# Scores of an attention kernel: one full matmul of mixed products and one of 64 rows, with two heads' tiles in turns

## The chip, the cores and the metric

The kernel runs on one core of a Trainium2 chip. A core has five engines that run side by side and wait for each other through semaphores: TensorE (matmuls, PE in the profile, with its weight loads as PEld), VectorE (DVE), ScalarE (ACT), GpSimd (POOL) and SyncE (SP), which here issues the DMAs. The metric is the device time of one execution in microseconds (us); lower is better.

## The reference

Attention with normalised queries and keys, and an MLP with an ELU on its result:

```python
B, H, S, D = 8, 12, 448, 64            # batches, heads, sequence, head size
q_n, k_n = rmsnorm(q, g_q), rmsnorm(k, g_k)
scores = (q_n @ k_n.T) / 8             # per batch and head, 448 x 448
attn = softmax(scores)                 # with the row maximum taken off
x = (attn @ v)                         # heads side by side: 3584 x 768
h = x @ w_in                           # 768 x 2048
g = where(h > 0, h, exp(min(h, 0)) - 1)
out = g @ w_out                        # 2048 x 768
```

All inputs are float32.

## The kernel before

Matmuls run in float16. To keep the precision of float32, each operand is split in a high part (its float16 value) and a low part (what is left), and several products of parts are added up in PSUM.

The work goes by pairs of heads p, 48 in all (6 for each batch). For a pair, `load_qk` fetches queries and keys, the `qk_...` steps normalise them, and `k_high`, `q_high`, `k_low`, `q_low` write high and low parts side by side into the tile `t16`, whose slots (query or key, 7 blocks of 128 rows, high or low, 64 values) become partitions when `qk_transpose` (line 439) transposes them by DMA into `qkt`. There, entry 0 has the queries and entry 1 the keys, head after head, with the high part in partitions 0 to 63 and the low part in 64 to 127. `q_swap` (line 446) moves the two halves of the queries into entry 2 with their places exchanged, by two more DMAs.

Scores are made by `s_mm(T)` in tiles T of 128 query rows, 7 for a pair (896 rows). Six tiles have rows of one head; one straddles both and is made of 64 rows of each (`cuts`). The list `ORDER` says which chunk of rows a tile takes: here 0, 1, 2, 4, 3, 5, 6, so the straddling chunk 3 is the fifth. A tile takes two matmuls over all 128 partitions (line 554): queries in entry 0 against keys give high by high plus low by low, and the exchanged ones in entry 2 give the mixed products. For the straddling tile each of them is two matmuls with 64 output partitions. The result is in one of the PSUM banks `s0` to `s4`, chosen by `t_s(T)`: five in turns at first, four once the MLP needs `s4`.

A tile is then worked on in steps: `s_max` (VectorE, line 561), `s_exp` (ScalarE, 575), `s_z` (GpSimd, 579), `s_rec` (VectorE, 587), `s_hi` (ScalarE, 618) and `s_lo` (VectorE, 628), which write high and low probabilities and free the bank, and `s_tr` (638), a DMA that transposes them. In pairs 1, 3 and 5 TensorE does this turning instead (`s_pe`, 599; there the low part is line 625). `attend(p)` (658) multiplies by the values, in matmuls of 64 output partitions for each head, in turns.

The MLP (`mlp`, lines 743 and 757, 128 x 448 outputs, two high by part and one low by high product) is a stream of matmuls that is laid between the attention's. The order of all is written out by hand: a loop over half steps h runs, at each h, the steps that the table `SCHED` puts there, and then part of the MLP's stream, by the targets of `due(h)`. With two things on TensorE in a half step, the stream's share is divided around them: from `START` on, `s_mm(T + 1)` comes at the odd half steps, and `attend(p - 1)` right behind the straddling tile of pair p:

```python
        if ok(T + 1) and odd == (h >= START):
            mm.append(lambda: s_mm(T + 1))
        if r == 7 and 0 <= p - 1 < NP:
            mm = [lambda mm=mm: (*(fn() for fn in mm), attend(p - 1))]
```

The order in which each engine meets its instructions is the order of this loop. The steps of tile T stand at 2T and following half steps; `s_lo` has 2T + 4.5. `PB` is 42, the tiles of a batch, and `NJ` is 7. In the first batch's attention the weights are converted and split as well (`conv_in`, `conv_out`), and no MLP is there yet.

Of the kernel before, what the change touches and what calls it, by code (L numbers as in the profile page):

```python
# [13 lines left out]
AF = mybir.ActivationFunctionType  # L14
ALU = mybir.AluOpType
# [4 lines left out]
B, H, S, D = 8, 12, 448, 64  # L20
# [3 lines left out]
NJ = 2 * S // 128  # L24
NCHUNK = B * NPAIR * NJ
PB = NPAIR * NJ
# [6 lines left out]
def tile_attention_then_elu_mlp(ctx: ExitStack, tc: tile.TileContext, qk, v, v_scan, gg, w_in, w_out, out):  # L33
# [13 lines left out]
    nc = tc.nc  # L47
# [8 lines left out]
    def bank(name):  # L56
        return psum.tile([128, 512], F32, name=name)

    sb = [bank(f"s{i}") for i in range(5)]
# [2 lines left out]
    taken = 0  # L62

    def t_s(T):
        return sb[T % (5 if T < PB + (5 if PE_PAIRS else 0) else 4)]

    def t_mo():
        nonlocal taken
# [9 lines left out]
        out=neg, in0=ident, scalar1=-1.0, scalar2=None, op0=ALU.mult  # L78
# [3 lines left out]
        out=ident, in0=ident, scalar1=2.0**UP, scalar2=None, op0=ALU.mult  # L82
# [260 lines left out]
    nat, vt, qkt, pts, pss, p16s, stats = ({} for _ in range(7))  # L343
    st1, sqs, t16s = {}, {}, {}
# [72 lines left out]
        )  # L417

    def q_high(p):
        nc.scalar.activation(t16s[p][:, 0, :, 0], nat[p][:, 0], AF.Copy)  # L420

    def k_low(p):
        t = t16s[p][:, 1]
# [4 lines left out]
    def q_low(p):  # L428
        t = t16s[p][:, 0]
        eng = nc.gpsimd if p else nc.vector  # L430
        eng.tensor_tensor(
            out=t[:, :, 1], in0=nat[p][:, 0], in1=t[:, :, 0], op=ALU.subtract
        )

    def qk_transpose(p, i):
# [4 lines left out]
            out=qkt[p][:, i], in_=t16[:, i].rearrange("p j s d -> p (j s d)")  # L440
        )

    def q_swap(p):
        q = qkt[p]
        for a, z in ((64, 0), (0, 64)):
            nc.sync.dma_start(out=q[z : z + 64, 2], in_=q[a : a + 64, 0])

    def v_mult(p):
        n = vn[p]
# [85 lines left out]
    def cuts(j):  # L535

        a, z = j * 128, j * 128 + 128
        if z <= S:
            return [(0, 0, a, 128)]
        if a >= S:  # L540
            return [(1, 0, a - S, 128)]
        return [(0, 0, a, S - a), (1, S - a, 0, z - S)]


    ORDER = (0, 1, 2, 4, 3, 5, 6)

    def s_mm(T):
        p, j = divmod(T, NJ)
        ps = pss[T] = t_s(T)
        qq = qkt[p].rearrange("p t j n -> p t (j n)")  # L550
        for t in (0, 2):
            for h, r0, q0, n in cuts(ORDER[j]):
                lhs = qq[:, t, h * S + q0 : h * S + q0 + n]
                nc.tensor.matmul(  # L554
                    ps[r0 : r0 + n, :S], lhs, qq[:, 1, h * S : h * S + S],
                    start=(t == 0), stop=(t == 2),
                )

    def s_max(T):
        st = stats[T] = small("st", 3, bufs=6)  # L560
# [4 lines left out]
    def by_pe(T):  # L565


        return T // NJ in PE_PAIRS
# [35 lines left out]
    def turned(T):  # L604
        q0 = ORDER[T % NJ] * 128
        ps = pss[T][:CK].rearrange("p (c q) -> p c q", c=4)
        return ps, pt_pe[:, 0, :, q0 : q0 + 128], pt_pe[:, 1, :, q0 : q0 + 128]
# [24 lines left out]
    def s_tr(T):  # L632
        p, j = divmod(T, NJ)
        p16 = p16s.pop(T)
        for h, r0, q0, n in cuts(ORDER[j]):
            if 2 * p + h not in pts:
# [150 lines left out]
    for T in reversed(range(NCHUNK)):  # L787
        k = 2 if by_pe(T) else 0 if T < PB else 1
        hs = [2 * T + h for h in SCHED["tile"][k]]
        j = T % NJ  # L790
# [7 lines left out]
    for p in range(NP):  # L798
        k = p if p < 12 else 11
        put([h + HP * (p - k) for h in SCHED["qk"][k]], [  # L800
            (load_qk, p), (qk_square, p), (qk_sum, p), (qk_root, p), (qk_newton, p), (qk_norm, p),
            (k_high, p), (q_gain, p), (q_high, p), (k_low, p), (q_low, p), (qk_transpose, p, 0),
            (qk_transpose, p, 1), (q_swap, p),
        ])
        put([h + HP * (p - k) for h in SCHED["v"][k]], [
            (load_v, p), (v_mult, p), (v_high, p), (v_low, p), (v_shift, p), (x_high, p),
            (x_low, p),
        ])
    for b in range(B):
        k = min(b, 2)  # L810
# [8 lines left out]
    for b in range(B):  # L819
        k = min(b, 1)  # L820
# [23 lines left out]
    for h in range(H0, LAST):  # L844
        T, odd = divmod(h, 2)

        run_tasks(h - 0.5, 1)
        run_tasks(h - 0.5, 2)
        run_tasks(h, 0)
        ok = lambda t: 0 <= t < NCHUNK  # L850
        run_tasks(h, 1)
        want = due(h + 1)
        n = max(0, want - done)
        mm = []
        p, r = divmod(h, HP)
# [5 lines that stand above are left out]
        parts = len(mm) + 1  # L861
        for k in range(parts):
            for _ in range(n * (k + 1) // parts - n * k // parts):
                r = next(moe, None)
                done += 1
                if r:
                    steps_at(h + 1, enumerate(r))
            if k < len(mm):
                mm[k]()
        run_tasks(h, 2)  # L870
    h = LAST - 1
# [106 lines left out]
PE_PAIRS = (1, 3, 5)  # L978
# [42 lines left out]
```

## Time and profile before

| | |
|---|---|
| time, median of 3 runs | 1267.01 us (1266.6 to 1267.09) |
| profiled execution, first to last instruction (its own time; nothing else of it is told) | 1265.7 us |
| TensorE busy, and its weight loads | 94%, 58% |
| VectorE, ScalarE, GpSimd busy | 68%, 70%, 43% |
| share of the DMA engines | 73% |
| score matmuls of 64 output columns of weights, of 128 | 192, 576 |

In the views below, a row of a timeline has the start in us from the span's start, the length, the engine, the line of the kernel, the operation, what it writes and reads, the shape, and how many are merged (x4); brackets show idle time of the engine just before, and what ended it. For a matmul, 128\*64 means 128 rows (contracted) by 64 columns of weights. A matmul's length is from its start until its last result; the next may start long before that end. A row of windows has the stretch, its length, and busy times. In a row of waits, the three numbers are the total in us, the count, and the longest.

### The profile page before, as it was taken

The numbers are of one execution on the slowest core, as the hardware profiler recorded it, in microseconds if no ns is written. First come the engines' busy times: TensorE is split into PE (matmuls) and PEld (weight loads), VectorE is DVE, ScalarE is ACT, GpSimd is POOL, SyncE is SP. The second block draws the span as 40 slices with busy tenths as digits, with TensorE's granted clock in tenths as the row PEclk, the third lists the DMA queues.
The fourth block names the chain that finished last, engine by engine and source line by source line (L and its number), as shares of the span: only waits on it lengthen the run. The fifth ranks groups of instructions, "written<-read, shape, count | busy, mean of one in ns | idle before, by whom it ended". The sixth has DMA issues, their size and how long they took to land.

```text
span 1265.7 us, 21796 instructions
## 1 busy us (share of the span) xinstructions
PE 1194.4 (94%) x7150; PEld 732.5 (58%) x7150; DVE 855.3 (68%) x1913; ACT 879.8 (70%) x1889; POOL 538.9 (43%) x858
## 2 busy tenths in 40 slices
PE   3777688999999999999999999999999999999998
PEld 2445444567556665576556755666557755675576
DVE  7999999986676667755785667755876668642310
ACT  6898789975797568854896578756886579643510
POOL 4776977674434433443434443334334343320000
PEclk9889799999999999999999999999999999999999
DMA  9987788989777876789577976799677968663012
GB/s 298 241 174 196 195 190 214 214 208 231 156 156 155 227 164 156 151 197 208 139 163 163 236 155 154 150 214 195 143 152 181 222 142 157 138 156 75 1 48 63
DMA packets 432978, 214.44 MB, mean 169 GB/s; under 512 B 389088, under 2 KB 409184, under 8 KB 432864
## 3 DMA queue, kind: packets, MB, share of 16 engines
q1 hardware_dynamic: 432864, 213.04, 73.4%
q8 instruction: 57, 0.93, 0.3%
q14 instruction: 57, 0.47, 0.1%
HBM read 93.52 MB, written 14.16 MB: 85 GB/s over the span
## 4 chain that ended last, share of the span: by engine, by line
PE 80%; DVE 6%; ACT 2%; issue 1%; POOL 1%; DMA 1%; SPq 0%; ACTq 0%; POOLq 0%
PE m L757 23%; PE m L743 20%; PE s L757 11%; PE s L743 10%; PE s L554 8%; PE av L658 7%; DVE gall L698 1%; DVE st L561 1%; DVE p L628 1%; DVE wts L243 1%; DVE w32s L267 1%; DVE e L690 1%; DMA qkt<-t 0%; POOL w32s L331 0%; ACT w32s L238 0%
## 5 line engine op out<-in xcount | busy, mean ns | idle before, releaser
L561 DVE TENSOR_REDUCE st<-s 128x1 f32<-128x448 f32 x336 | 208.7, 621 | 207.8 <-PE s L554 206.6
L579 POOL TENSOR_SCALAR st<-st 128x1 f32<-128x1 f32 x336 | 86.2, 257 | 483.8 <-ACT s L575 467.7
L757 PE MATMUL m<-gall,whos 128*128 128x448 f16 x1024 | 283.1, 353 | 0.0
L743 PE MATMUL m<-x,whi 128*128 128x448 f16 x1020 | 281.8, 353 | 0.8 <-DVE x L669 0.8
L757 PEld LDWEIGHTS <-whos 128*128 128x128 f16 x1536 | 221.9, 145 | 74.0 <-issue 1.1
L618 ACT ACTIVATE p<-s,st 128x448 f16<-128x448 f32 x294 | 186.2, 633 | 80.3 <-DMA pt<-p 47.6
L575 ACT ACTIVATE s<-s,st 128x448 f32<-128x448 f32 x315 | 190.6, 605 | 63.6 <-DVE st L561 62.8
L743 PEld LDWEIGHTS <-whi 128*128 128x128 f16 x1536 | 149.3, 98 | 136.0 <-issue 1.3
L628 DVE SCALAR_TENSOR_TENSOR p<-s,st,p 128x448 f16<-128x448 f32 x294 | 199.1, 677 | 15.2 <-ACT p L618 14.9
L554 PE MATMUL s<-qkt 128*128 128x448 f16 (+1 forms) x768 | 185.6, 362 | 21.8 <-DVE gall L625 14.5
L757 PE MATMUL m<-gall,wls 128*128 128x448 f16 x512 | 181.1, 354 | 0.0
L743 PE MATMUL m<-x,wli 128*128 128x448 f16 x510 | 179.9, 353 | 0.0
L743 PE MATMUL s<-x,whi 128*128 128x448 f16 x516 | 141.7, 352 | 0.0
L757 PE MATMUL s<-gall,whos 128*128 128x448 f16 x512 | 141.6, 353 | 0.0
L757 PEld LDWEIGHTS <-wls 128*128 128x128 f16 x768 | 110.4, 144 | 41.3 <-issue 6.7
L743 PEld LDWEIGHTS <-wli 128*128 128x128 f16 x768 | 75.1, 98 | 75.8 <-issue 8.2
L554 PEld LDWEIGHTS <-qkt 128*128 128x128 f16 (+1 forms) x768 | 62.9, 101 | 89.2 <-issue 48.5
L698 DVE SCALAR_TENSOR_TENSOR gall<-e,gsc,gall 128x448 f16<-128x448 f32 x128 | 96.2, 752 | 24.4 <-ACT gall L695 24.4
L658 PE MATMUL av<-pt,vt 128*64 128x448 f16 x990 | 101.5, 353 | 1.0 <-DMA raws<-in_w_out 1.0
L695 ACT ACTIVATE gall<-e,gsc 128x448 f16<-128x448 f32 x128 | 85.2, 665 | 18.0 <-DVE e L690 17.7
L686 ACT ACTIVATE e<-e,nisc,isc 128x448 f32<-128x448 f32 x128 | 96.9, 757 | 0.3
L665 ACT ACTIVATE x<-av 128x448 f16<-128x448 f32 x48 | 26.0, 542 | 99.2 <-PE av L658 65.6
(120 smaller groups left out, 1774.3 us busy)
## 6 DMA issues: line engine op xcount, KB each, us to landing
wls<-wl_d SPq DMA_DIRECT2D x48, 512.0 KB, 4.1
nat<-in_qk SPq DMA_DIRECT2D x48, 448.0 KB, 3.6
raws<-in_w_out SPq DMA_DIRECT2D x24, 512.0 KB, 4.5
qkt<-qkt SPq DMA_DIRECT2D x96, 112.0 KB, 2.3
out<-y SPq DMA_DIRECT2D x48, 224.0 KB, 2.9
vn<-in_v SPq DMA_DIRECT2D x38, 256.0 KB, 3.3
vscan<-in_v_scan SPq DMA_DIRECT2D x36, 224.0 KB, 3.9
whos<-in_w_in SPq DMA_DIRECT2D x10, 768.0 KB, 7.0
```

What stands on the lines that cost most here:

```text
L554: nc.tensor.matmul(ps[r0 : r0 + n, :S], lhs, qq[:, 1, h * S : h * S + S], start=(t == 0), stop=(t == 2),)
L561: nc.vector.tensor_reduce(out=st[:, 0:1], in_=pss[T][:, :S], axis=AX.X, op=ALU.max, negate=True)
L575: nc.scalar.activation(e, ps, AF.Exp, bias=st[:, 0:1], accum_out=st[:, 1:2])
L579: nc.gpsimd.tensor_scalar(out=st[:, 1:2], in0=st[:, 1:2], scalar1=1e-9, scalar2=2.0 ** (UP - 7) if by_pe(T) else 2.0**-7, op0=ALU.add, op1 ...
L618: nc.scalar.activation(p16[:, :S], pss[T][:, :S], AF.Copy, scale=stats[T][:, 2:3])
L628: nc.vector.scalar_tensor_tensor(out=p16[:, S:], in0=ps[:, :S], scalar=r, in1=p16[:, :S], op0=ALU.mult, op1=ALU.subtract)
L658: nc.tensor.matmul(av[64 * h : 64 * h + 64, :S], vs[:, h], ps[h], start=(k == 0), stop=(k == len(terms) - 1),)
L686: nc.scalar.activation(e, e, AF.Identity, scale=isc, bias=nisc)
L695: nc.scalar.activation(g[:, 0], e, AF.Copy, scale=gsc)
L698: nc.vector.scalar_tensor_tensor(out=g[:, 1], in0=e, scalar=gsc, in1=g[:, 0], op0=ALU.mult, op1=ALU.subtract)
L743: nc.tensor.matmul(ph[:, :S], w[:, c, :], x[:, r, :], start=(c == 0 and i == 0), stop=last)
L757: nc.tensor.matmul(py[:, :S], w, g[:, r, :], start=(f == 0 and i == 0), stop=last)
```

## The change

The query parts change their slots: high goes to slot 1 and low to slot 0, so that in `qkt` the queries have low above high while the keys keep high above low. One matmul over 128 partitions now gives both mixed products (`s_cross`), straight from entries 0 and 1. The product high by high takes 64 partitions (`s_high_high`): for head 0 partitions 0 to 63, for head 1 partitions 64 to 127. Entry 2 now holds, in one block of 448 columns, the high queries of head 0 (moved to partitions 0 to 63) and the high keys of head 1 (moved to 64 to 127). Low by low is no longer computed. `ORDER` puts tiles of the two heads in turns. From pair 7 on, for the tiles beside the straddling one, the first of two issues its mixed matmul, its high by high matmul, and behind it the high by high matmul of the second, into the second's bank; the second issues only its mixed matmul, two half steps later. In pairs 0 to 6, and in every straddling tile, a tile issues mixed and high by high products by itself. The rule for the banks is changed to go on in the same rotation when five become four.

```diff
     def t_s(T):
-        return sb[T % (5 if T < PB + (5 if PE_PAIRS else 0) else 4)]
+        return sb[T % 5 if T < PB + 5 else (T + 3) % 4]
...
-        nc.scalar.activation(t16s[p][:, 0, :, 0], nat[p][:, 0], AF.Copy)
+        nc.scalar.activation(t16s[p][:, 0, :, 1], nat[p][:, 0], AF.Copy)
...
-            out=t[:, :, 1], in0=nat[p][:, 0], in1=t[:, :, 0], op=ALU.subtract
+            out=t[:, :, 0], in0=nat[p][:, 0], in1=t[:, :, 1], op=ALU.subtract
...
+    def highs(p):
+        return qkt[p][:, 2].rearrange("p j n -> p (j n)")[:, :S]
+
+    def of_head(p, t, h):
+        return qkt[p][:, t].rearrange("p j n -> p (j n)")[:, h * S : h * S + S]
+
     def q_swap(p):
-        q = qkt[p]
-        for a, z in ((64, 0), (0, 64)):
-            nc.sync.dma_start(out=q[z : z + 64, 2], in_=q[a : a + 64, 0])
+        for h in (0, 1):
+            a = 64 - 64 * h
+            nc.sync.dma_start(out=highs(p)[64 * h : 64 * h + 64], in_=of_head(p, h, h)[a : a + 64])
...
-    ORDER = (0, 1, 2, 4, 3, 5, 6)
+    ORDER = (0, 4, 1, 5, 3, 2, 6)
+
+    def paired(T):
+        return T >= PB + NJ and T % NJ != 4
+
+    def second_of(T):
+        return paired(T) and T % NJ in (1, 3, 6)
+
+    def s_cross(T):
+        p, j = divmod(T, NJ)
+        second = second_of(T)
+        for h, r0, q0, n in cuts(ORDER[j]):
+            nc.tensor.matmul(
+                pss[T][r0 : r0 + n, :S], of_head(p, 0, h)[:, q0 : q0 + n], of_head(p, 1, h),
+                start=not second, stop=second,
+            )
+
+    def s_high_high(T):
+        p, j = divmod(T, NJ)
+        second = second_of(T)
+        for h, r0, q0, n in cuts(ORDER[j]):
+            rows = slice(64 * h, 64 * h + 64)
+            q = of_head(p, 0, h) if h else highs(p)
+            k = highs(p) if h else of_head(p, 1, h)
+            nc.tensor.matmul(
+                pss[T][r0 : r0 + n, :S], q[rows, q0 : q0 + n], k[rows], start=second,
+                stop=not second,
+            )
 
     def s_mm(T):
-        p, j = divmod(T, NJ)
-        ps = pss[T] = t_s(T)
-        qq = qkt[p].rearrange("p t j n -> p t (j n)")
-        for t in (0, 2):
-            for h, r0, q0, n in cuts(ORDER[j]):
-                lhs = qq[:, t, h * S + q0 : h * S + q0 + n]
-                nc.tensor.matmul(
-                    ps[r0 : r0 + n, :S], lhs, qq[:, 1, h * S : h * S + S],
-                    start=(t == 0), stop=(t == 2),
-                )
+        if second_of(T):
+            s_cross(T)
+            return
+        pss[T] = t_s(T)
+        s_cross(T)
+        s_high_high(T)
+        if paired(T):
+            pss[T + 1] = t_s(T + 1)
+            s_high_high(T + 1)
```

## The prediction

> **What bounds the kernel now.** I read the page's busy table, slices and chain first, then busy time by stage, then who waits for whom in each stage, then single rows of TensorE.
>
> ```profile
> PE 1194.4 (94%) x7150; PEld 732.5 (58%) x7150; DVE 855.3 (68%) x1913; ACT 879.8 (70%) x1889; POOL 538.9 (43%) x858
> PE   3777688999999999999999999999999999999998
> PE 80%; DVE 6%; ACT 2%; issue 1%; POOL 1%; DMA 1%; SPq 0%; ACTq 0%; POOLq 0%
> ```
>
> TensorE is at nine tenths or more from the eighth slice (31.6 us each) on, and has 80% of the chain that ended last. An average of 94% says little; the stages say where an added TensorE nanosecond counts.
>
> ```profile
> 0.00:50.00 50.00, 23.09 (x151) 12.75 (x152) 41.33 (x91) 35.72 (x73) 26.25 (x34) 0.90 0.98 261
> 50.00:100.00 50.00, 40.98 (x302) 24.66 (x298) 44.35 (x93) 43.99 (x100) 36.53 (x54) 0.90 0.90 218
> 100.00:150.00 50.00, 34.78 (x268) 23.12 (x267) 48.91 (x110) 41.02 (x92) 37.70 (x53) 0.86 0.78 196
> 150.00:200.00 50.00, 41.30 (x301) 22.84 (x300) 46.64 (x98) 44.00 (x93) 38.40 (x47) 0.97 0.82 189
> 200.00:250.00 50.00, 43.69 (x304) 23.79 (x303) 48.56 (x100) 47.61 (x100) 34.54 (x42) 1.00 0.87 210
> 250.00:271.00 21.00, 19.57 (x125) 13.98 (x123) 20.83 (x42) 17.28 (x38) 15.61 (x21) 1.00 0.86 215
> 271.00:400.00 129.00, 129.00 (x764) 77.64 (x764) 92.82 (x215) 95.86 (x209) 56.85 (x96) 1.00 0.78 179
> 900.00:1136.00 236.00, 236.00 (x1369) 144.35 (x1368) 153.89 (x353) 166.93 (x363) 89.30 (x161) 1.00 0.73 162
> ```
>
> Columns: length, then busy time of PE, PEld, DVE, ACT and POOL, the granted clock, DMA share, GB/s. Before 271 us VectorE is the fullest (20.83 of the last 21 us) and TensorE has 271 - 203.4 = 67.6 us of idle time. From 271 us to the last score tile near 1136 us TensorE has none (129.00 of 129, 236.00 of 236), while VectorE is at 65 to 72%. The score matmuls of that stage, with full-width and half-width forms as they stand in the whole run:
>
> ```profile
> 271.00:1138.00 867.00, 142.95 (x600) 49.17 (x600) 1.00 0.78 173
> L554 PE MATMUL s<-qkt 128*128 128x448 f16 x576 | 157.1, 356 | 19.1 <-DVE gall L625 11.8 <-DVE p L628 4.3 <-DVE gall L628 1.2
> L554 PE MATMUL s<-qkt 128*64 128x448 f16 x192 | 28.6, 379 | 2.7 <-DVE gall L625 2.7
> ```
>
> A head pair issues 16 score matmuls (12 full ones, 4 on 64 columns), so 600 of them are 37.5 of the 48 pairs: these lie where TensorE alone sets the time. Asked who waited there, TensorE answers with nothing; all its waits of the second and third row end before 271 us.
>
> **The change, part by part.** *What it takes away.* Six tiles of a pair have 128 rows of one head. Each took two full matmuls; now two such tiles take one full matmul each (mixed products) and a 64-row one each, in different halves of the array. The low by low product is dropped. If the two 64-row matmuls run together, two tiles take three turns instead of four. A turn, and the cost of a change of shape, come from these TensorE rows, where the same stream meets a full tile, then the straddling tile with its 64-column matmuls and the attention product:
>
> ```profile
> 710.99 0.54 PE L757 MATMUL s<-gall,whos 128*128 128x448 f16 x2
> 711.47 0.57 PE L554 MATMUL s<-qkt 128*64 128x448 f16 x4
> 711.87 2.25 PE L658 MATMUL av<-pt,vt 128*64 128x448 f16 x22
> 714.05 0.41 PE L757 MATMUL s<-gall,wls 128*128 128x448 f16 x1
> 714.29 0.54 PE L757 MATMUL s<-gall,whos 128*128 128x448 f16 x2
> 711.46 0.14 PEld L554 LDWEIGHTS <-qkt 128*64 128x64 f16 x4 [0.32 <-issue]
> 714.04 0.14 PEld L757 LDWEIGHTS <-wls 128*128 128x128 f16 x1 [0.36 <-issue]
> 641.60 0.54 PE L743 MATMUL s<-x,whi 128*128 128x448 f16 x2
> 642.07 0.57 PE L554 MATMUL s<-qkt 128*64 128x448 f16 x4
> 642.47 2.25 PE L658 MATMUL av<-pt,vt 128*64 128x448 f16 x22
> 644.65 0.36 PE L743 MATMUL s<-x,wli 128*128 128x448 f16 x1
> 644.85 0.54 PE L743 MATMUL s<-x,whi 128*128 128x448 f16 x2
> 647.12 0.54 PE L554 MATMUL s<-qkt 128*128 128x448 f16 x2
> 647.50 0.54 PE L743 MATMUL m<-x,whi 128*128 128x448 f16 x2
> ```
>
> The full score tile at 647.12 holds the array for 0.38 us, 0.19 a matmul. The 22 attention matmuls last 2.25 us: less the 0.35 us that any one shows, ten steps of 0.19, so two half-width matmuls in different columns do run together. But the stream does not go smoothly into that shape and back. The last full matmul before starts at 711.18 (710.99 and 0.19); 2 + 11 half-width turns and its own make 14 x 0.19 = 2.66, and the next full one starts at 714.05, 2.87 later: 0.21 lost, and 0.05 more before the next (714.29 is 0.24 later, not 0.19). By the other rows: 641.79 to 644.65 is 2.86, so 0.20, and 0.01 more. About 0.10 is lost at each border: in both directions the weight load, elsewhere done under the running matmul, comes only when the array stood idle for it ("issue", 0.32 and 0.36 us). So a visit to another shape costs 0.21 us (before a line 743 matmul) to 0.26 us (before 757); they alternate evenly, 0.235 us.
>
> [...]
>
> *What it adds.* The 64-row pair stands between full matmuls: three visits per pair. Bounds for one visit: 0, as between full matmuls, and 0.26, the dearer measured one; below 0 is excluded, since the 448 columns still take their 0.19. I take 0.235, by the nearest rows. Three tile pairs: 3 x (0.235 - 0.19) = +0.135 us.
>
> *The straddling tile.* Now two 64-column matmuls, then two of 64 rows by 64 columns, then the attention product in 64 columns as before: four half-units as before, but two more borders, one visit: +0.235 (0 to 0.26). Together +0.37 us per pair; times 37.5 is **+13.9 us** (bounds: -0.57 x 37.5 = -21.4 with free borders, and 4 x 0.26 - 0.57 = 0.47, +17.6).
>
> *The bank one tile earlier.* The second tile's 64-row matmul comes with the first tile, so its bank must be free one tile earlier: it now waits for the low probabilities (line 628, the bank's last reader) of three tiles back, not four. Where VectorE is behind, that is a wait, and the MLP matmuls of lines 743 and 757 queue behind it. The last such place before TensorE's unbroken stretch, and the tightest case found in that stretch:
>
> ```profile
> 276.24 0.54 PE L554 MATMUL s<-qkt 128*128 128x448 f16 x2
> 277.60 0.69 DVE L628 SCALAR_TENSOR_TENSOR p<-s,st,p 128x448 f16<-128x448 f32 x1
> 768.20 0.68 DVE L628 SCALAR_TENSOR_TENSOR p<-s,st,p 128x448 f16<-128x448 f32 x1
> 768.99 0.54 PE L554 MATMUL s<-qkt 128*128 128x448 f16 x2
> ```
>
> The tile at 276.24 is the first of two that will go together, and line 628 of three tiles back ends at 278.29. The early matmul would start some 0.3 us after 276.24, so it waits 1.8 us, which nothing behind can make up: **+1.8 us** (0 if VectorE has moved up, 5 if earlier waits add up). Near 769 us line 628 ends at 768.88, 0.4 us before the early matmul at 769.3, and that VectorE is a third idle there keeps it so.
>
> *The first seven pairs* (p below 7) are not paired: 64-row matmul and full one take turns, with no turn saved and 6 + 1 more visits each, 7 x 7 x 0.235 = 11.5 us, and 4 x 0.37 = 1.5 us for the four pairs up to 271 us. The cover is TensorE's 67.6 us of idle there. Who waited before 271 us:
>
> ```profile
> PE s L554 <- DVE gall L625: 14.5, 11, 2.7
> DVE st L561 <- PE s L554: 1.4, 1, 1.4
> ```
>
> TensorE waits for VectorE, almost never the reverse. I let 1.5 us through (0 to 5; all 13 without cover).
>
> *The copies.* Each of the two moves of a pair carries half the bytes (56 instead of 112 KB, 5.4 of 214 MB in all). DMA is full only before 100 us, where five pairs' saved 0.56 MB at some 240 GB/s are 2.3 us at most. But the second now reads the transposed keys, and waits on the sync queue for the later transposition:
>
> ```profile
> DMA to landing us min/median/max: 2.9/3.0/5.6
> 52.53 1.23 SPq L439 DMA_TRANSPOSE qkt<-t  x1
> 54.51 1.17 SPq L446 DMA_DIRECT2D qkt<-qkt  x2
> 55.73 1.09 SPq L229 DMA_DIRECT2D whos<-in_w_in  x2
> ```
>
> A transposition issued at 52.53 lands between 55.4 and 58.1; the second move went out near 55.1, so up to 3 us of queue time can go here, with weight loads behind it, and probability transpositions in other places. Early on I put it at +0.5 (-2 to 4); later the move is far ahead of its use. Moving high and low to the other slots, the head order of the tiles and the rotation of the banks (it goes on evenly from five banks to four) issue the same instructions on ScalarE, VectorE, GpSimd and the sync queue: nothing, since both heads' probability buffers come free with the same attention product before and after.
>
> Sum: 13.9 + 1.8 + 1.5 + 0.5 = +17.7 us on this execution's span of 1265.7, so 1283.4. The median of the runs, 1267.01, lies 1.3 us above that span: **1285 us**.
>
> **The rivals.** *Free borders (ends faster).* The 64-row halves need no idle array: their weights load under the running matmul, and a pair costs three plain turns. Then -21.4 + 1.8 + 1.5 + 0.5: 1249 us. For it: rows are not columns, and the lost 0.10 could come from the routing of columns alone. Against it: both directions show the loss, also back into the full shape. It decides at 4c = 0.57 less the other 3.8 us over 37.5 pairs, so c = 0.117 us per visit: half the measured price. [...]
>
> [...]
>
> *No overlap of the two halves.* Nothing in before shows two row halves at once. One after the other, each pair of tiles takes four turns again: 37.5 x 3 x 0.19 = 21.4 more, 1306 us.
>
> *One bank in the straddling tile.* Its two 64-row matmuls write different partitions of one bank. If they take turns, 0.19 more per pair: 7.1, 1292 us. For columns the same sharing costs nothing (four score matmuls in 0.57 us). [...]
>
> **How the numbers follow.** Forecast 0.52; free borders 0.22; half price 0.10, a little to either side; no overlap 0.08; one bank 0.08. A measurement here tells 0.2% (2.5 us) from no change. Faster: 0.22 and 0.04 of the half price, 0.26. Same: 0.05. Slower: 0.52, 0.08, 0.08 and 0.01, 0.69. The forecast's own range is 1272 (weights hidden, so visits of 0.19: pairs even, straddling tile 0.19 x 37.5 = 7, less the copies' 2) to 1296 (0.26 a visit, 17.6, and the early terms near their upper ends). The two signs both carry weight, so the range goes from 1247, the free borders, to 1296, and leaves out the missing overlap.
>
> **What would show it.** Right: around a 64-row pair, the full matmul, the pair and the next full matmul start some 0.29 us apart each, the pair's two starts a few ns apart, with "issue" idle in the weight loads; line 757 and 743 busy as before, and the stage from 271 us longer by some 14 us. Free borders would show steps of 0.19 and PE's end 20 us earlier; no overlap, two starts 0.19 apart; the bank, a wait of TensorE on line 628 between 176 and 290 us. I am wrong above all if 64 rows cost less than half of what 64 columns cost at the borders.

## The result, and the profile after

The changed kernel takes 1286.63 us (median of 4 runs, 1286.29 to 1287.67) against 1267.05 us (4 runs, 1266.6 to 1267.39): 1.0156 times as long, 95% interval 1.0141 to 1.017. 1285 us was forecast. The profiled execution has a span of 1285.0 us.

The page after, busy table, slices and chain (lines 743 and 757 are now 780 and 794, the attention product 695, the mixed products 566, the 64-row matmuls 579, the low probabilities 665):

```profile
PE 1222.9 (95%) x7150; PEld 708.7 (55%) x7150; DVE 857.8 (67%) x1913; ACT 881.2 (69%) x1889; POOL 535.1 (42%) x858
PE   4787699999999999999999999999999999999998
PE 81%; DVE 5%; ACT 2%; POOL 1%; issue 1%; DMA 1%; ACTq 0%; POOLq 0%; SPq 0%; DVEq 0%
```

As before, a turn is the 0.19 us for which a matmul, or two in different parts of the array, holds it; a border is a change from one shape of matmul to another, and a visit goes to another shape and back, over two borders. There are as many matmuls as before (7150), fewer turns by construction, and still 28.5 us more of busy TensorE. The span is 19.3 us longer: TensorE's idle time fell from 71.3 to 62.1 us, so some 9 us of the added work fell into time in which it had been idle. The matmuls of one pair of tiles, with the stream on both sides:

```profile
728.38 0.35 PE L794 MATMUL m<-gall,wls 128*128 128x448 f16 x1
728.57 0.35 PE L566 MATMUL s<-qkt 128*128 128x448 f16 x1
728.86 0.36 PE L579 MATMUL s<-qkt 64*128 64x448 f16 x2
729.15 0.60 PE L794 MATMUL m<-gall,whos 128*128 128x448 f16 x2
729.59 0.35 PE L794 MATMUL m<-gall,wls 128*128 128x448 f16 x1
```

The two 64-row matmuls run together (two of them take 0.36 us, as each of those that stand alone takes in the kernel with no tile paired, at 728.65 and 731.93). But 0.29 us lie between the starts of the full matmul and the pair, and 0.29 again to the next full one, where the stream has 0.19. The first matmul after the visit costs 0.06 more (729.15 and 0.25 to the second, then 0.19). From 728.38 to 729.59 there are five turns, 0.95 us, and 1.21 have passed: 0.26 for the visit, and one turn of 0.19 saved. Where the stream is that of line 780, the visit is cheaper:

```profile
657.72 0.35 PE L780 MATMUL m<-x,wli 128*128 128x448 f16 x1
657.91 0.35 PE L566 MATMUL s<-qkt 128*128 128x448 f16 x1
658.19 0.36 PE L579 MATMUL s<-qkt 64*128 64x448 f16 x2
658.49 0.55 PE L780 MATMUL m<-x,whi 128*128 128x448 f16 x2
658.88 0.35 PE L780 MATMUL m<-x,wli 128*128 128x448 f16 x1
```

Five turns again, and 1.16 us from 657.72 to 658.88: 0.21 for the visit. The mean of the two is 0.235.

The straddling tile, which led straight into the attention product before (0.40 us from its start to that product's), and the weight loads there:

```profile
722.76 0.54 PE L794 MATMUL s<-gall,whos 128*128 128x448 f16 x2
723.23 0.38 PE L566 MATMUL s<-qkt 128*64 128x448 f16 x2
723.54 0.38 PE L579 MATMUL s<-qkt 64*64 64x448 f16 x2
723.85 2.27 PE L695 MATMUL av<-pt,vt 128*64 128x448 f16 x22
723.54 0.11 PEld L579 LDWEIGHTS <-qkt 64*64 64x64 f16 x2 [0.20 <-issue]
723.85 1.84 PEld L695 LDWEIGHTS <-vt 128*64 128x64 f16 x22 [0.20 <-issue]
```

Now 0.62 us, and the product itself 2.27 instead of 2.25: 0.24 more. At both of these changes of shape the weight load comes late ("issue", 0.20 us of nothing before it).

```profile
653.24 2.27 PE L695 MATMUL av<-pt,vt 128*64 128x448 f16 x22
```

This attention product is three pairs ahead of the one at 723.85: 70.61 us. Before, the same two stood at 642.47 and 711.87, 69.40 us apart. These three pairs got 0.40 us longer each; two of them have the dearer stream of line 794. Three pairs further on, first before, then after:

```profile
781.40 2.25 PE L658 MATMUL av<-pt,vt 128*64 128x448 f16 x22
794.44 2.27 PE L695 MATMUL av<-pt,vt 128*64 128x448 f16 x22
```

Over six pairs, half with each stream, 138.93 us became 141.20: 0.38 us a pair, 14.2 us for 37.5 pairs.

### The profile page after: what moved, and what is told of

It is laid out like the page before. It is cut to its first block, busy times and chain, and to the rows that moved or that the text cites. A ratio compares the mean times of both kernels' runs of the same rounds, so it can differ in the third digit from the quotient of the medians.

```text
span 1285.0 us, 21777 instructions
## 1 busy us (share of the span) xinstructions
PE 1222.9 (95%) x7150; PEld 708.7 (55%) x7150; DVE 857.8 (67%) x1913; ACT 881.2 (69%) x1889; POOL 535.1 (42%) x858
## 4 chain that ended last, share of the span: by engine, by line
PE 81%; DVE 5%; ACT 2%; POOL 1%; issue 1%; DMA 1%; ACTq 0%; POOLq 0%; SPq 0%; DVEq 0%
PE m L794 23%; PE m L780 20%; PE s L794 11%; PE s L780 10%; PE av L695 7%; PE s L566 4%; PE s L579 4%; DVE gall L735 1%; DVE p L665 1%; DVE st L598 1%; DVE w32s L267 1%; DVE wts L243 1%; DMA pt<-p 0%; DVE e L727 0%; DMA raws<-in_w_out 0%
## 5 line engine op out<-in xcount | busy, mean ns | idle before, releaser
L566 PE MATMUL s<-qkt 128*128 128x448 f16 (+1 forms) x384 | 121.2, 363 | 14.6 <-DVE gall L662 13.4
L735 DVE SCALAR_TENSOR_TENSOR gall<-e,gsc,gall 128x448 f16<-128x448 f32 x128 | 99.3, 776 | 24.4 <-ACT gall L732 24.4
L780 PE MATMUL s<-x,wli 128*128 128x448 f16 x258 | 91.3, 354 | 0.0
```

The lines of the kernel that those rows point to most:

```text
L566: nc.tensor.matmul(pss[T][r0 : r0 + n, :S], of_head(p, 0, h)[:, q0 : q0 + n], of_head(p, 1, h), start=not second, stop=second,)
L735: nc.vector.scalar_tensor_tensor(out=g[:, 1], in0=e, scalar=gsc, in1=g[:, 0], op0=ALU.mult, op1=ALU.subtract)
L780: nc.tensor.matmul(ph[:, :S], w[:, c, :], x[:, r, :], start=(c == 0 and i == 0), stop=last)
```

## The experiments

All times below are medians beside runs of the kernel before on the same chip (1267.35 us for the first four, 1267.39 for the other three).

**All rows, bank opened early.** It takes the borders away and leaves all else of the change.

```diff
-            rows = slice(64 * h, 64 * h + 64)
-            q = of_head(p, 0, h) if h else highs(p)
-            k = highs(p) if h else of_head(p, 1, h)
+            rows = slice(0, 128)
+            q = of_head(p, 0, h)
+            k = of_head(p, 1, h)
```

> The changed kernel with every 64-row matmul replaced by one over all 128 rows (it repeats the mixed product, so high by high is left out of the scores). Order of the tiles, copies and the bank opened one tile early stay; TensorE issues as many score matmuls and turns as before the change, and never changes to 64 rows. Theory (borders): the 233 ns a visit and 239 ns a pair for the straddling tile are gone, so only what is not borders stays: 1267 plus 2 to 6 us, that is 1269 to 1273 us; from the eleventh attention product on, 617 ns steps between pairs as before (23.1 us a pair). Rival (the early bank, the copies or the order cost the 19 us): about 1286 us.

Measured: 1272.18 us, ratio 1.0033 (1.0021 to 1.0046). The borders less the saved turns are worth the difference to the changed kernel, 14.4 us. The rest, 4.8 us, is not borders. A pair takes 23.1 us again (69.39 for three; no row here shows the 617 ns of the expectation):

```profile
645.52 2.25 PE L695 MATMUL av<-pt,vt 128*64 128x448 f16 x22
714.91 2.25 PE L695 MATMUL av<-pt,vt 128*64 128x448 f16 x22
```

**All rows, each tile in its own time.** The edit above, and this:

```diff
     def paired(T):
-        return T >= PB + NJ and T % NJ != 4
+        return False
```

> As the one before, and no tile opens its bank early: each issues its two 128-row matmuls by itself. What is left of the change is the tiles' order, the copies and the bank rotation. If the early bank makes the 5 us lost between the eighth and the eleventh attention product, this one lies at 1267 plus or minus 1 us and the one before 3 to 5 us above it; if borders in the stretch where VectorE is full make them, both lie within 1 us of 1267; if copies or order make them, both lie near 1272.

Measured: 1267.63 us, ratio 1.0002 (0.9993 to 1.0011). Order, copies and bank rotation together cost nothing that can be told; the early bank costs the 4.6 us between the medians of this kernel and the last (4.1 us between their profiled spans, 1264.9 and 1269.0). Of the waits of TensorE between 160 and 300 us, those for the bank's readers, first of the kernel with the early bank, then of this one:

```profile
PE s L579 <- DVE p L665: 10.8, 8, 2.0
PE s L566 <- DVE gall L662: 2.7, 1, 2.7
```

```profile
PE s L566 <- DVE p L665: 3.8, 3, 1.5
PE s L566 <- DVE gall L662: 2.7, 1, 2.7
```

Eight waits for the low probabilities instead of three, and 7 us more of them: the second tile's early matmul stands at the bank while VectorE is behind.

**No tile paired.** Only the edit of `paired`, with 64 rows.

> The changed kernel with no tile paired: each of the six one-head tiles makes its 64-row matmul alone, in its own visit. Theory (borders): per pair 6 visits of 0.233 us with no turn saved and 0.239 for the straddling tile, 1.64 us, times 37.5 pairs is 61 us on 1267, and 0 to 5 us before: 1328 to 1333 us. Rival (the early bank costs the time): no bank is opened early, so it lies below the changed kernel, near 1270 to 1286 us.

Measured: 1330.87 us, ratio 1.0498 (1.0482 to 1.0514). Twice the visits and no turn saved cost what the price says, although no bank is opened early any more.

**The straddling tile over all rows.** The pairs of tiles stay as changed.

```diff
-            rows = slice(64 * h, 64 * h + 64)
-            q = of_head(p, 0, h) if h else highs(p)
-            k = highs(p) if h else of_head(p, 1, h)
+            wide = T % NJ == 4
+            rows = slice(0, 128) if wide else slice(64 * h, 64 * h + 64)
+            q = of_head(p, 0, h) if h or wide else highs(p)
+            k = highs(p) if h and not wide else of_head(p, 1, h)
```

> The changed kernel with the straddling tile's second product over all 128 rows (it repeats the mixed product there, so high by high is left out in these 64 plus 64 rows). Theory (borders): its two inner borders go, 0.239 us a pair, 9.0 us in all: 1277 to 1278 us. Rival (the inner borders are hidden by the attention product behind them, or the loss lies in the pairs alone): within 1 us of 1286.6.

Measured: 1278.6 us, ratio 1.0085 (1.0071 to 1.0099): 8.0 us less than the changed kernel, 9.0 expected, and 0.6 us above the range of 1277 to 1278. Its rows around the tile:

```profile
720.37 0.38 PE L566 MATMUL s<-qkt 128*64 128x448 f16 x2
720.58 0.35 PE L580 MATMUL s<-qkt 128*64 128x448 f16 x2
720.77 2.25 PE L696 MATMUL av<-pt,vt 128*64 128x448 f16 x22
```

0.40 us from the tile to the product, as before the change: without the third shape there is no loss.

**Both halves from the same rows.**

```diff
-            rows = slice(64 * h, 64 * h + 64)
+            second_half = h == 1 and T % NJ == 4
+            rows = slice(64, 128) if second_half else slice(0, 64)
```

> The changed kernel with the 64-row matmul of head 1's tiles read from partitions 0 to 63 too (the high queries of head 0 in place of head 1's keys, so those tiles' high by high product is wrong data). Both matmuls of a pair of tiles then use the same half of the array. Theory (the halves run together only because their rows differ): they take turns, 3 x 0.19 us a pair more, 37.5 x 0.57 = 21 us on 1286.6, that is 1307 us, with two starts 0.19 us apart in the rows. Rival (TensorE runs two short-row matmuls together anyway, or the weight loads cover it): within 2 us of 1286.6.

Measured: 1309.04 us, ratio 1.0334 (1.0318 to 1.0351).

```profile
722.66 0.35 PE L566 MATMUL s<-qkt 128*128 128x448 f16 x1
722.95 0.55 PE L580 MATMUL s<-qkt 64*128 64x448 f16 x2
723.43 0.41 PE L795 MATMUL m<-gall,whos 128*128 128x448 f16 x1
```

Two matmuls now end 0.55 us after the first began, not 0.36: they take turns, 0.20 us apart, and the 22 us more (21 expected) are the turns that the change saves. Between the two, which have the same shape, nothing else is lost.

**One visit, beside the attention product.** If each border has its price, a visit that takes the place of an existing border is cheaper. This kernel is the one before, with one pair of 64-row matmuls per pair of heads, from pair 13 on (after the stretch where the early bank costs):

```diff
+        if p >= FROM:                                   # in q_swap; FROM = 13
+            q = q.rearrange("p t j n -> p t (j n)")
+            nc.sync.dma_start(out=moved(p)[64:128], in_=q[0:64, 1, S : 2 * S])
...
-    ORDER = (0, 1, 2, 4, 3, 5, 6)
+    ORDER = (0, 1, 4, 2, 3, 5, 6)
...
+        if p >= FROM and j in (3, 5):                   # in s_mm
+            if j == 3:
+                pss[T] = t_s(T)
+            h, _, q0, _ = cuts(ORDER[j])[0]
+            nc.tensor.matmul(
+                pss[T][:, :S], qq[:, 2, h * S + q0 : h * S + q0 + 128],
+                qq[:, 1, h * S : h * S + S], start=(j == 3), stop=(j == 5),
+            )
+            return
+        if p >= FROM and j == 4:                        # ahead of the straddling tile
+            pss[T + 1] = t_s(T + 1)
+            for U, rows, t, k in (
+                (T - 1, slice(0, 64), 0, qq[:, 1, :S]), (T + 1, slice(64, 128), 2, moved(p))
+            ):
+                h, _, q0, _ = cuts(ORDER[U % NJ])[0]
+                nc.tensor.matmul(
+                    pss[U][:, :S], qq[rows, t, h * S + q0 : h * S + q0 + 128], k[rows],
+                    start=(U > T), stop=(U < T),
+                )
...
+        late_by = [1.5, 1.5, 1.5, 1, 0.5, 0.5, 0.5, 0.5, 0.5]
...
+        if j == 3 and T // NJ >= FROM:                  # steps of the fourth tile
+            hs = [h + d for h, d in zip(hs, late_by)]
```

(`moved(p)` is room that the weight conversion no longer needs)

> The kernel before the change, with its full products, but from pair 13 on two tiles of a pair (the fourth and the sixth) leave low by low out: their 64-row matmuls run together once, placed right in front of the straddling tile and the attention product, where the stream changes its shape anyway. The fourth tile's later steps come up to 1.5 half steps later, the sixth tile's bank is opened one tile early, and a third copy brings head 1's high keys to partitions 64 to 127. Theory (price by borders): one turn of 0.19 us less, one border of 0.10 us more and 0.01 to 0.03 of weights, 0.07 to 0.08 us a pair gained, times 35 pairs: 2.4 to 3.0 us, 1264 to 1265 us. Rival (a visit costs 0.23 us wherever it stands): 0.04 x 35 = 1.5 us slower, 1268 to 1269 us. Rival (later steps and early bank stall TensorE): 1267 or more, with waits for line 628 in the rows.

**The same with full rows**, as its control:

```diff
-                    pss[U][:, :S], qq[rows, t, h * S + q0 : h * S + q0 + 128], k[rows],
+                    pss[U][:, :S], qq[:, 0, h * S + q0 : h * S + q0 + 128],
+                    qq[:, 1, h * S : h * S + S],
```

> The one before with these two matmuls over all 128 partitions (high by high with low by low), so no 64-row shape and no turn saved; copies, banks and steps the same. Every theory of the borders: 1267 plus or minus 1 us; if the moved steps or the early bank cost something, it shows here alone, above 1268 us. The difference to the one before is what the 64 rows bring there.

Measured: 1265.58 us with the visit, ratio to before 0.9988 (0.9979 to 0.9997); 1268.07 us without, ratio 1.0007 (0.9997 to 1.0016). The 64 rows bring 2.5 us against the control, within the 2.4 to 3.0 expected. Against the kernel before, 1.8 us are left, less than expected (1265.58 against 1264 to 1265): the kernel with the visit beats both kernels, but by 0.12% only. The control lies 0.7 us above the kernel before, which its interval does not tell from nothing; TensorE's one wait in it between 300 and 400 us is for low probabilities:

```profile
PE s L573 <- DVE p L655: 0.4, 1, 0.4
```

First the rows with the visit, then the control's:

```profile
710.37 0.54 PE L783 MATMUL s<-gall,whos 128*128 128x448 f16 x2
710.84 0.36 PE L573 MATMUL s<-qkt 64*128 64x448 f16 x1
710.85 0.36 PE L573 MATMUL s<-raws,qkt 64*128 64x448 f16 x1
711.14 0.57 PE L580 MATMUL s<-qkt 128*64 128x448 f16 x4
711.54 2.25 PE L684 MATMUL av<-pt,vt 128*64 128x448 f16 x22
```

```profile
712.04 0.54 PE L784 MATMUL s<-gall,whos 128*128 128x448 f16 x2
712.42 0.54 PE L573 MATMUL s<-qkt 128*128 128x448 f16 x2
712.89 0.57 PE L581 MATMUL s<-qkt 128*64 128x448 f16 x4
```

From the last full matmul of the stream (710.56; 712.23) to the straddling tile pass 0.58 us, against 0.66: 0.08 us a pair, with three borders around the attention where the control has two.

## Why the prediction was right, point by point

*TensorE sets the time from 271 us on.* Borne out. In the stage after, TensorE is nearly as unbroken as before, from 300 us on; the first row below is the hand-over, and the 0.07 us of idle time in the last row come up again under the early bank.

```profile
271.00:300.00 29.00, 27.55 (x171) 18.06 (x171) 19.95 (x54) 15.66 (x35) 16.30 (x25) 1.00 0.93 214
300.00:400.00 100.00, 100.00 (x582) 53.48 (x579) 68.40 (x154) 74.61 (x162) 37.43 (x64) 1.00 0.68 156
400.00:900.00 500.00, 500.00 (x2857) 293.42 (x2855) 329.49 (x763) 342.30 (x752) 196.01 (x345) 1.00 0.76 169
900.00:1136.00 236.00, 235.93 (x1347) 133.03 (x1346) 159.13 (x355) 169.95 (x369) 90.15 (x159) 1.00 0.72 157
```

*A visit of 64 rows costs what one of 64 columns costs, 0.235 us.* This was the open step, taken by the nearest rows, and it held: 0.26 before line 794 and 0.21 before line 780, as the two column visits of before. The rival of free borders fell with the 0.29 us steps in the rows, and with the all-rows kernel, which is faster than the one with fewer turns; half price (near 0.12 a visit) fell with the same rows. What happens inside the array in the 0.10 us of a border no run shows.

*The straddling tile, +0.235 us a pair.* 0.24 by the rows, 8.0 of the 8.8 us by the experiment.

*A pair, +0.37 us.* 0.38 over six pairs, 14.2 us for 37.5 where 13.9 was forecast. For the whole run the borders less the turns, forecast at 13.9 with 1.5 for the early pairs, are the difference between the changed kernel and the one with all rows: 14.4 us between the medians, 16.0 between the profiled spans (1285.0 and 1269.0). What the early pairs cost by themselves was not measured; that TensorE's idle time fell by 9 us fits with most of their 11.5 us being covered.

*The early bank, +1.8 us.* The mechanism held and the size was too small: 4.6 us. The prediction counted only the last wait before TensorE's unbroken stretch, as the one that nothing behind makes up. In the runs the waits before 300 us added up, towards the 5 us that stood as the upper bound. TensorE's waits for low probabilities between 160 and 300 us, first before, then in the changed kernel:

```profile
PE s L554 <- DVE p L628: 4.3, 4, 1.5
PE s L579 <- DVE p L665: 8.9, 7, 1.7
```

Its rows at one later place, VectorE's first:

```profile
952.28 0.67 DVE L665 SCALAR_TENSOR_TENSOR p<-s,st,p 128x448 f16<-128x448 f32 x1
952.29 0.35 PE L566 MATMUL s<-qkt 128*128 128x448 f16 x1
952.57 0.78 PE L579 MATMUL s<-qkt 64*128 64x448 f16 x2
953.28 0.36 PE L780 MATMUL s<-x,whi 128*128 128x448 f16 x1
```

Here, in the unbroken stretch, a pair of 64-row matmuls is drawn out to 0.78 us: the second began near 953.00, just after the low probabilities ended at 952.95. The first had ended 0.07 us earlier. So the second stood for its bank once here, 0.43 us late, although the tightest case that the prediction found in this stretch, near 769 us, had 0.4 us to spare. How far the lost time before 300 us is TensorE's waits themselves and how far VectorE's own delay through them was not separated.

*The copies, +0.5 us.* The wait on the sync queue is there, and as long as was put down for the worst case, 3 us:

```profile
51.06 1.22 SPq L439 DMA_TRANSPOSE qkt<-t  x1
53.01 4.29 SPq L453 DMA_DIRECT2D qkt<-qkt  x2
57.35 1.05 SPq L229 DMA_DIRECT2D whos<-in_w_in  x2
```

Two moves hold the queue for 4.29 us instead of 1.17, with weight loads behind them. It costs nothing that shows: the kernel with order, copies and bank rotation alone is at 1.0002.

*The bank of the straddling tile.* The two matmuls of 64 rows and 64 columns write different partitions of one bank and run together (two in 0.38 us, above; in turns they would take 0.35 and 0.19, about 0.54 us), so this rival fell. No run here has them write the same partitions.

*No overlap of the halves.* Fell: 0.36 us for two, and 22 us more when they must take turns.

The forecast came within 2 us with one term clearly mis-sized. The early bank came out higher than its 1.8 us by 2.8 between the medians and by 2.3 between the profiled spans. The other terms together came out lower by 0.9 between the medians and by 0.7 between the spans, but which of them did is not settled: borders and early pairs, 15.4 forecast, are 14.4 or 16.0. Single runs of one kernel lie 2 us and more apart (1266.79 to 1269.05 us in the kernel before), so how near the total came is partly luck; the price of a border, which the rows show, is not.

## What to carry to other kernels

Before packing short matmuls into parts of the array, read the price of a change of shape from a place where the stream already makes one, and count borders, not matmuls: here a visit costs 0.20 to 0.26 us and saves 0.19. Put an odd shape beside a border that is there anyway, where it adds one border instead of two (0.11 us here, for the 0.19 of the turn saved). And a bank taken one tile early costs where its reader is the bound, 4.6 us here, even if it is nearly free in the steady state (the rows above show one such wait there, of 0.43 us, at 952.57).

## What the runs showed of the hardware

A border costs much the same, 0.09 to 0.12 us, wherever one shape follows another in these rows: full to 64 columns (722.95, the second of two at 722.76, to 723.23, 0.09 over a turn), full to 64 rows (728.57 to 728.86, 0.10), 64 rows back to full (728.86 to 729.15), 64 rows to 64 columns (710.84 to 711.14, 0.11), and 64 columns to 64 rows by 64 columns (723.23 to 723.54, 0.12). So a visit between two different shapes, with a border there anyway, adds one border, not two (0.20 us lost from 710.56 to 711.14, where the control loses 0.09 from 712.23 to 712.89), while the 64 rows by 64 columns of the straddling tile, put inside a stretch of 64 columns, added two (0.62 us to the attention product instead of 0.40). Between two matmuls of 64 rows by 128 columns none is lost, even if they must take turns (0.20 us apart with the same rows).
